# A fused attention and ReGLU block on one Trainium2 core: one load of activations cut into four pieces on two DMA queues

## The chip, the cores and the metric

The kernel runs on one core of one Trainium2 chip. A core has a matrix engine (TensorE, PE in the profile), a vector engine (VectorE, DVE), an engine for activations (ScalarE, ACT), GpSimd (POOL) and an engine that mainly issues DMAs (SyncE, SP). PEld is TensorE's weight load. Each engine works through its own list of instructions in order. The metric is the device time of one execution in microseconds (us), lower being better. The time before is 204.27 us, the median of 4 runs (202.77 to 205.07).

## The reference: what is computed

For 2048 rows x of 512 bf16 numbers, a layer norm, an attention with 32 heads of 16 numbers over 8 keys at distances 0, 2, ..., 14, a residual, a second layer norm and a gated feed-forward block with 1376 inner columns:

```
h  = x + A(layernorm(x), wqkv, wo)       # A: qkv = x @ wqkv; softmax over 8 dilated keys; @ wo
g  = layernorm(h) @ W_gate;  u = layernorm(h) @ W_up
h2 = h + (relu(g) * u) @ W_down
```

## The kernel before: stages, queues and order

The 2048 rows are four chunks of 512 rows (tk 0 to 3), and each chunk is four blocks of 128 rows (j 0 to 3). All of x lives in one tile `x_sm` with 16 blocks; chunk 1 is blocks 4 to 7. For each chunk the kernel takes the layer norm (statistics on VectorE at L419 and L422, the reciprocal root on ScalarE at L432 and L436, the normalised rows on VectorE at L454), transposes the rows (TensorE at L483 with evictions at L497 on VectorE and L499 on ScalarE, or by DMA at L472), multiplies with `wqk_sb` and `wv_sb` (L524, evicted by ScalarE at L532), does the attention (products on VectorE at L571 and L659 with additions by DMA at L691, sums and spreads on TensorE at L577 and L638), multiplies with `wo_sb` (L711), and does the feed-forward block (L749, L753, L756, L769, L786, L797).

The order of all this work on each engine is fixed: `Plan.order` sorts the steps by a list of ranks written out by hand (`RANK`), and nothing of it depends on when a load lands. Loads enter that plan only as assumed landing times. The loads themselves, and some constants, are emitted by `setup()`, ahead of every step of the plan. For the steps of this case, `setup()` puts out, in order of the program:

- four loads of 128 rows each for chunk 0, even blocks on SP's queue and odd blocks on ACT's (L282);
- the four 128-row slabs dt 0 to 3 of the query and key weights `wqk_sb`, even slabs on SP's queue and odd slabs on ACT's (L284);
- one load of 512 rows for chunk 1 on SP's queue (L285);
- the load of ScalarE's function table (L286), which stands on ScalarE's list after its four DMA issues;
- constants on GpSimd, then two copies of one number that act as gates: the copy at L299 reads the first block of chunk 0, and the load of `wv_sb` (L300) follows it; the copy at L301 reads the first block of chunk 1, block 4, and the load of chunk 2 (L303) follows it;
- on SP's queue then chunk 3 (L303), `wo_sb` (L305), `wu_sb` (L306), `wg_sb` (L307), `wd_sb` (L308, L311).

The tool that builds the program signals the landings of DMAs of both hardware queues (SP's and ACT's) on eight semaphores, taken in rotation in the order in which the DMAs stand in the program. A DMA therefore waits, on the engine that issues it, until the DMA eight places before it in that order has landed. In the program of before, places 1 to 8 are the four loads of chunk 0 (ACT's block 1, SP's block 0, ACT's block 3, SP's block 2) and the four slabs (dt 1, dt 0, dt 3, dt 2). The load of chunk 1 is place 9 and waits for block 1; `wv_sb` is place 10 and waits for block 0; chunk 2 and chunk 3 wait for blocks 3 and 2; `wo_sb` waits for dt 1, and so on.

On TensorE the list begins with 44 warm-up products (L373), the transposes of blocks 0 and 1, 16 filler products (L381), the first four products of L524 (one for each slab dt 0 to 3, on 256 columns), and the transposes of blocks 3 and 2 between further products. On VectorE the statistics of chunk 1 (L419) come after the eviction L497 of block 3; block 7 is the first of them, then blocks 6, 5 and 4.

Of the kernel before, what the change touches and what calls it, by code (L numbers as in the profile page):

```python
# [187 lines left out]
def kernel(  # L188
# [11 lines left out]
    nc = tc.nc  # L200
# [16 lines left out]
    BPC = CS // P  # L217
# [4 lines left out]
    x_rows = A_x.rearrange("b (tb p) d -> p (b tb) d", p=P)  # L222
# [20 lines left out]
    x_sm = sb.tile([P, NTB, D], BF16, name="x_sm")  # L243
# [34 lines left out]
    def setup():  # L278

        w3_r = A_wqkv.rearrange("(dt p) f -> p dt f", p=P)  # L280
        for j in range(BPC):
            (nc.scalar if j % 2 else nc.sync).dma_start(x_sm[:, j:j + 1, :], x_rows[:, j:j + 1, :])  # L282
        for dt in range(NT):
            (nc.scalar if dt % 2 else nc.sync).dma_start(wqk_sb[:, dt:dt + 1, :], w3_r[:, dt:dt + 1, 0:2 * D])  # L284
        nc.sync.dma_start(x_sm[:, BPC:2 * BPC, :], x_rows[:, BPC:2 * BPC, :])  # L285
        nc.scalar.preload_act_table_set("natural_log_exp_and_others")  # L286
        V.memset(warm[:], 0.0)
        make_identity(nc, identity[:])
        nc.gpsimd.memset(eps_t[:], EPS)
        nc.gpsimd.iota(ci[:], pattern=[[0, 1]], base=0, channel_multiplier=1)  # L290
        nc.gpsimd.iota(sel_i[:], pattern=[[1, H]], base=0, channel_multiplier=0)
        nc.gpsimd.iota(sp_i[:], pattern=[[1, H], [0, DQ]], base=0, channel_multiplier=0)
        nc.gpsimd.iota(sm_i, pattern=[[0, 4], [1, H]], base=0, channel_multiplier=0)
        nc.gpsimd.iota(mk_i[:], pattern=[[1, PADL]], base=0, channel_multiplier=0)
        nc.gpsimd.memset(kT[:, :, 0:PADL], 0.0)
        nc.gpsimd.memset(vT[:, :, 0:PADL], 0.0)


        nc.gpsimd.tensor_copy(out=wv_sb[0:1, 0, 0:1], in_=x_sm[0:1, 0, 0:1])  # L299
        nc.sync.dma_start(wv_sb[:], w3_r[:, :, 2 * D:3 * D])  # L300
        nc.gpsimd.tensor_copy(out=x_sm[0:1, 2 * BPC, 0:1], in_=x_sm[0:1, BPC, 0:1])  # L301
        for tk in range(2, NCK):
            nc.sync.dma_start(x_sm[:, tk * BPC:(tk + 1) * BPC, :], x_rows[:, tk * BPC:(tk + 1) * BPC, :])  # L303

        nc.sync.dma_start(wo_sb[:], A_wo.rearrange("(p t) f -> p t f", t=NT))  # L305
        nc.sync.dma_start(wu_sb[:], B_W_up.rearrange("(dt p) f -> p dt f", p=P))  # L306
        nc.sync.dma_start(wg_sb[:], B_W_gate.rearrange("(dt p) f -> p dt f", p=P))  # L307
        nc.sync.dma_start(  # L308
            wd_sb[:, 0:NFF, :], B_W_down[0:NFF * P, :].rearrange("(ft p) n -> p ft n", p=P))
        if FTAIL:  # L310
            nc.sync.dma_start(wd_sb[:FTAIL, NFF, :], B_W_down[NFF * P:F, :])  # L311


        for n, (op, by) in enumerate(((ALU.arith_shift_right, 2), (ALU.bitwise_and, H - 1),
                                      (ALU.arith_shift_right, 5))):
            V.tensor_scalar(out=tmp[:, n:n + 1], in0=ci[:], scalar1=by, scalar2=None, op0=op)
        V.tensor_copy(out=cf[:, 0:3], in_=tmp[:])
        V.tensor_scalar(out=cf[:, 2:3], in0=cf[:, 2:3], scalar1=1.0 * DIL, scalar2=None, op0=ALU.mult)
        V.tensor_scalar(out=cf[:, 3:4], in0=cf[:, 2:3], scalar1=4.0 * DIL, scalar2=None, op0=ALU.add)
        V.tensor_scalar(out=sel[:], in0=sel_i[:], scalar1=cf[:, 0:1], scalar2=None, op0=ALU.is_equal)  # L320
        V.tensor_scalar(out=spread[:], in0=sp_i[:], scalar1=cf[:, 1:2], scalar2=None, op0=ALU.is_equal)
        V.tensor_scalar(out=same[:], in0=sm_i, scalar1=cf[:, 1:2], scalar2=None, op0=ALU.is_equal)
        for hf in range(2):
            V.tensor_scalar(out=mask[:, hf, :], in0=mk_i[:], scalar1=cf[:, 2 + hf:3 + hf],
                            scalar2=None, op0=ALU.is_ge)
# [488 lines left out]
    with tc.manual_schedule():  # L814
        setup()
        for op in todo:
            if op.fn is not None:
                op.fn()
# [35 lines left out]
```

## Time and profile before

| what | value |
|---|---|
| median of 4 runs | 204.27 us (202.77 to 205.07) |
| the profiled execution's own time | 205.07 us |
| its span, first to last instruction | 203.3 us |
| mean granted TensorE clock | 0.994 |
| TensorE busy | 193.6 us, 95% of the span |
| VectorE busy | 153.3 us, 75% |
| ScalarE busy | 121.8 us, 60% |
| GpSimd busy | 12.7 us, 6% |
| load of chunk 1, issue to landing | 7.0 us |
| load of `wv_sb`, issue to landing | 7.9 us |

Lines such as L285 are line numbers of the kernel. In a timeline a row has the start, the busy time, the engine, the line, the operation, what it writes and reads, how many instructions were merged into the row, and in brackets how long the engine sat idle before it and what ended that. An engine name with a q (SPq, ACTq) is the engine's sequencer: it issues a DMA, and the time is that of the issue and not of the transfer. In the chain of work that ended last, each row has a start, a duration and what carried the chain then. A row of waits has the waiting instruction, what it waited for, the total in us, how many times, and the longest.

### The profile page before, as it was taken

The numbers are of one execution on the slowest core, as the hardware profiler recorded it, in microseconds if no ns is written. First come the engines' busy times: TensorE is split into PE (matmuls) and PEld (weight loads), VectorE is DVE, ScalarE is ACT, GpSimd is POOL, SyncE is SP. The second block draws the span as 40 slices with busy tenths as digits, with TensorE's granted clock in tenths as the row PEclk, the third lists the DMA queues.
The fourth block names the chain that finished last, engine by engine and source line by source line (L and its number), as shares of the span: only waits on it lengthen the run. The fifth ranks groups of instructions, "written<-read, shape, count | busy, mean of one in ns | idle before, by whom it ended". The sixth has DMA issues, their size and how long they took to land.

```text
span 203.3 us, 2938 instructions
## 1 busy us (share of the span) xinstructions
PE 193.6 (95%) x1095; PEld 96.1 (47%) x1115; DVE 153.3 (75%) x239; ACT 121.8 (60%) x256; POOL 12.7 (6%) x28
## 2 busy tenths in 40 slices
PE   8799999989999999999999999999999999999990
PEld 8576446545445434444444444444444444444460
DVE  6689998989999999999996768799958313023240
ACT  3367698746899966787436779601568511477300
POOL 3000000420000013100131000000000000000000
PEclk9999999999999999999999999999999999999997
DMA  5969962895000009920399400221010130200103
GB/s 150 351 193 380 401 191 53 150 206 108 3 0 0 0 3 175 194 44 3 63 177 191 118 0 0 50 53 55 0 52 0 26 77 3 77 0 0 52 6 100
DMA packets 17677, 18.83 MB, mean 93 GB/s; under 512 B 8352, under 2 KB 14464, under 8 KB 17664
## 3 DMA queue, kind: packets, MB, share of 16 engines
q1 hardware_dynamic: 15360, 11.57, 18.4%
q0 software_dynamic: 1728, 6.29, 16.4%
q10 hardware_dynamic: 576, 0.79, 1.4%
q8 instruction: 9, 0.15, 0.3%
q14 instruction: 4, 0.03, 0.0%
HBM read 8.42 MB, written 2.10 MB: 52 GB/s over the span
## 4 chain that ended last, share of the span: by engine, by line
PE 65%; DVE 15%; DMA 8%; ACT 5%; SPq 2%; issue 2%; ACTq 0%
PE bank L749 28%; PE bank L524 15%; PE bank L786 14%; DVE big L659 6%; PE bank L711 5%; DMA quad<-row 4%; DMA wqk_sb<-in_A_wqkv_dram 4%; DVE big L571 3%; DVE gT L769 2%; SPq L472 1%; DVE x_sm L722 1%; DVE big L662 1%; PE bank L577 1%; PE bank L483 1%; ACT big L644 1%
## 5 line engine op out<-in xcount | busy, mean ns | idle before, releaser
L749 PE MATMUL bank<-quad,wu_sb 128*128 128x512 bf16 (+1 forms) x172 | 42.4, 379 | 0.4
L749 PE MATMUL bank<-quad,wg_sb 128*128 128x512 bf16 (+1 forms) x173 | 42.0, 379 | 0.3 <-DMA quad<-row 0.3
L756 ACT ACTIVATE gr<-bank 128x512 bf16<-128x512 f32 (+1 forms) x44 | 25.4, 618 | 24.7 <-PE bank L749 22.9
L786 PE MATMUL bank<-wd_sb,gT 128*128 128x512 bf16 (+2 forms) x183 | 39.8, 366 | 0.2
L753 ACT CAST up_sb<-bank 128x512 bf16<-128x512 f32 (+1 forms) x44 | 25.1, 602 | 21.0 <-PE bank L749 17.3
L571 DVE TENSOR_TENSOR big<-quad,kT 128x4096 bf16<-128x4096 bf16 x16 | 36.2, 2285 | 0.2
L659 DVE TENSOR_TENSOR big<-big,vT 128x4096 bf16<-128x4096 bf16 x16 | 35.9, 2282 | 0.0
L769 DVE TENSOR_TENSOR gT<-gr,up_sb 128x1024 bf16<-128x1024 bf16 (+1 forms) x24 | 15.3, 642 | 24.0 <-ACT up_sb L753 14.4
L524 PE MATMUL bank<-quad,wqk_sb 128*128 128x512 bf16 (+1 forms) x139 | 30.2, 355 | 2.1 <-DMA wqk_sb<-in_A_wqkv_dram 1.0
L786 PEld LDWEIGHTS <-gT 128*128 128x128 bf16 (+1 forms) x187 | 18.1, 98 | 19.7 <-issue 0.4
L749 PEld LDWEIGHTS <-wg_sb 128*128 128x128 bf16 (+1 forms) x176 | 17.3, 100 | 21.1 <-issue 0.9
L749 PEld LDWEIGHTS <-wu_sb 128*128 128x128 bf16 (+1 forms) x176 | 17.5, 100 | 20.6 <-issue 0.7
L524 PEld LDWEIGHTS <-wqk_sb 128*128 128x128 bf16 x144 | 15.6, 114 | 14.1 <-issue 2.4
L797 DVE TENSOR_TENSOR row<-x_sm,bank 128x512 bf16<-128x512 bf16 (+1 forms) x17 | 10.6, 649 | 10.4 <-PE bank L786 10.4
L644 ACT CAST big<-bank 128x512 bf16<-128x512 f32 x32 | 17.8, 641 | 0.4 <-PE bank L638 0.2
L662 DVE TENSOR_TENSOR big<-big 128x1024 bf16<-128x1024 bf16 (+2 forms) x24 | 16.8, 728 | 0.1
L691 POOL DMA_DIRECT2D big<-big x12 | 10.5, 872 | 87.9 <-DVE big L659 59.9
L524 PE MATMUL bank<-quad,wv_sb 128*128 128x512 bf16 x62 | 15.6, 380 | 0.2
L711 PE MATMUL bank<-wo_sb,quad 128*128 128x512 bf16 x62 | 15.2, 379 | 0.2
L454 DVE TENSOR_SCALAR row<-x_sm,mv,rs 128x512 bf16<-128x512 bf16 x32 | 11.4, 407 | 3.7 <-ACT rs L436 3.1
L499 ACT COPY quad<-bank 128x1024 bf16<-128x1024 bf16 (+1 forms) x9 | 8.0, 931 | 7.2 <-PE bank L483 7.2
L532 ACT CAST quad<-bank 128x512 bf16<-128x512 f32 x16 | 9.5, 614 | 4.6 <-PE bank L524 4.6
(68 smaller groups left out, 147.2 us busy)
## 6 DMA issues: line engine op xcount, KB each, us to landing
big<-big POOLq DMA_DIRECT2D x12, 512.0 KB, 5.5
out_dram<-row SPq DMA_DIRECT2D x15, 128.0 KB, 1.8
x_sm<-in_A_x_dram SPq DMA_DIRECT2D x3, 512.0 KB, 5.8
wu_sb<-in_B_W_up_dram SPq DMA_DIRECT2D x1, 1376.0 KB, 9.7
wg_sb<-in_B_W_gate_dram SPq DMA_DIRECT2D x1, 1376.0 KB, 12.8
wd_sb<-in_B_W_down_dram SPq DMA_DIRECT2D x1, 1280.0 KB, 16.0
wqk_sb<-in_A_wqkv_dram ACTq DMA_DIRECT2D x2, 256.0 KB, 6.5
wqk_sb<-in_A_wqkv_dram SPq DMA_DIRECT2D x2, 256.0 KB, 6.7
```

The lines of the kernel that those rows point to most:

```text
L454: V.tensor_scalar(out=xn.t[:], in0=x, scalar1=mv.t[:, j, 0:1], scalar2=rs.t[:, j:j + 1], op0=ALU.add if residual else ALU.subtract, op1=AL ...
L524: nc.tensor.matmul(mm.t[:, lo:hi], lhsT=wv_sb[:, dt, t:D:NT] if c == 2 else wqk_sb[:, dt, c * D + t:(c + 1) * D:NT], rhs=xnT.t[:, dt, lo:h ...
L571: V.tensor_tensor(out=pb.t[:].rearrange("p (t w) s -> p t w s", t=2), in0=q4, in1=k4, op=ALU.mult)
L644: nc.scalar.copy(out=ab.t[:, w, :], in_=bc.t[:])
L659: V.tensor_tensor(out=mt.t[:], in0=ab.t[:], in1=v8, op=ALU.mult)
L662: V.tensor_tensor(out=mt.t[:, 0:n, :], in0=mt.t[:, 0:n, :], in1=mt.t[:, n:2 * n, :], op=ALU.add)
L711: nc.tensor.matmul(od.t[:], lhsT=OT.t[:, t, j * P:(j + 1) * P], rhs=wo_sb[:, t, :], start=(t == 0), stop=(t == NT - 1 and tk not in RPE))
L749: nc.tensor.matmul(mm.t[:fs, :], lhsT=w_sb[:, dt, ft * P: ft * P + fs], rhs=hnT.t[:, dt, :], start=(dt == 0), stop=(dt == NT - 1))
L753: nc.scalar.copy(out=ub.t[:fs, i, :], in_=um.t[:fs, :])
L756: nc.scalar.activation(out=gr.t[:fs, i, :], in_=gm.t[:fs, :], func=ACT.Relu)
L769: V.tensor_tensor(out=gt.t[:fs, 0:n, :], in0=gr.t[:fs, 0:n, :], in1=ub.t[:fs, 0:n, :], op=ALU.mult)
L786: nc.tensor.matmul(od.t[:, c0:c1], lhsT=gts[ft].t[:fs, ft % 2, j * P:(j + 1) * P], rhs=wd_sb[:fs, ft, c0:c1], start=(ft == 0), stop=(ft == ...
```

## The change

The single load of chunk 1 is replaced by four loads of one block (128 rows, 128 KB) each. Blocks 4 and 6 go to SP's queue and blocks 5 and 7 to ACT's. The place in `setup()` is the same: after the slabs of `wqk_sb` and before the table load. The bytes are the same, and nothing else of the kernel is edited.

```
@@ -282,7 +282,8 @@
             (nc.scalar if j % 2 else nc.sync).dma_start(x_sm[:, j:j + 1, :], x_rows[:, j:j + 1, :])
         for dt in range(NT):
             (nc.scalar if dt % 2 else nc.sync).dma_start(wqk_sb[:, dt:dt + 1, :], w3_r[:, dt:dt + 1, 0:2 * D])
-        nc.sync.dma_start(x_sm[:, BPC:2 * BPC, :], x_rows[:, BPC:2 * BPC, :])
+        for j in range(BPC, 2 * BPC):
+            (nc.scalar if j % 2 else nc.sync).dma_start(x_sm[:, j:j + 1, :], x_rows[:, j:j + 1, :])
         nc.scalar.preload_act_table_set("natural_log_exp_and_others")
         V.memset(warm[:], 0.0)
         make_identity(nc, identity[:])
```

More of the change, by code (lines that the diff above doesn't have):

```diff
@@ L284, in setup @@
             (nc.scalar if dt % 2 else nc.sync).dma_start(wqk_sb[:, dt:dt + 1, :], w3_r[:, dt:dt + 1, 0:2 * D])
-        nc.sync.dma_start(x_sm[:, BPC:2 * BPC, :], x_rows[:, BPC:2 * BPC, :])
+        for j in range(BPC, 2 * BPC):
+            (nc.scalar if j % 2 else nc.sync).dma_start(x_sm[:, j:j + 1, :], x_rows[:, j:j + 1, :])
         nc.scalar.preload_act_table_set("natural_log_exp_and_others")
```

## The prediction, made before the change was run

> **What bounds the kernel now.** I read the chain of work that ended last first, since the change touches only the first 20 us and the question is what carries the end there.
>
> ```profile
> 2.16 7.12 DMA wqk_sb<-in_A_wqkv_dram
> 9.28 0.05 issue
> 9.32 0.41 PE bank L524 x2
> 9.73 0.22 PE bank L483 x4
> ...
> 31.49 0.86 PE bank L524 x4
> 32.35 0.24 PE bank L483 x4
> 32.59 0.03 issue
> 32.62 0.42 DVE row L454
> ```
>
> The load of slab dt 2, issued by SP at 2.16, lands at 9.28 and starts TensorE's third product of L524. From there to 32.6 every row is TensorE's but for hops of 0.05, so whatever moves that product moves everything up to there; the chain then goes on through work in a fixed order to the end. No row names the load of chunk 1.
>
> Next the timeline from 0 to 20 us, for what stands around that load:
>
> ```profile
> 2.61 1.28 ACT L286 ACT_TABLE_LOAD   x1 [2.61 <-issue]
> ...
> 3.45 0.39 SPq L285 DMA_DIRECT2D x_sm<-in_A_x_dram  x1
> ...
> 3.95 0.46 SPq L300 DMA_DIRECT2D wv_sb<-in_A_wqkv_dram  x1
> ...
> 4.63 0.29 ACT L432 ACTIVATE rs<-mv,eps_t 128x1 f32<-128x1 f32 x1 [0.73 <-DVE mv L422]
> ...
> 6.83 1.06 PE L381 MATMUL bank<-warm 128*128 128x128 bf16 x16
> ...
> 7.92 0.41 PE L524 MATMUL bank<-quad,wqk_sb 128*128 128x256 bf16 x2
> ...
> 9.32 0.41 PE L524 MATMUL bank<-quad,wqk_sb 128*128 128x256 bf16 x2 [0.99 <-DMA wqk_sb<-in_A_wqkv_dram]
> ...
> 9.99 0.42 DVE L497 COPY quad<-bank 128x512 bf16<-128x512 bf16 x1 [1.56 <-PE bank L483]
> ...
> 10.51 2.47 DVE L419 BATCH_NORM_STATS2 st<-x_sm 128x6 f32<-128x512 bf16 x4
> 10.54 0.18 POOL L301 COPY x_sm<-x_sm 1x1 bf16<-1x1 bf16 x1 [6.71 <-DMA x_sm<-in_A_x_dram]
> ...
> 10.74 1.41 SPq L303 DMA_DIRECT2D x_sm<-in_A_x_dram  x2
> ```
>
> Three things are in it. The load of chunk 1 lands at 3.45 + 7.0 = 10.45; its reader, L419, starts at 10.51, directly behind L497 (9.99 + 0.42 = 10.41), with no idle time noted. So the landing and VectorE's arrival coincide, and VectorE's arrival was set by TensorE, which was set by dt 2. TensorE has a hole of 0.99 us before 9.32, and VectorE one of 1.56 before 9.99: chunk 0's layer norm is early by about 1 us. And ScalarE's table load starts at 2.61, as its fourth DMA issue ends; the first layer norm step of chunk 0 on ScalarE follows at 4.63, 0.73 after the table load.
>
> Last the waits of SP's queue:
>
> ```profile
> SPq L285 <- DMA x_sm<-in_A_x_dram: 0.8, 1, 0.8
> ```
>
> L285 reads nothing that an earlier load writes, yet SP stood 0.8 us, until block 1 (issued 0.73, 2.7 to landing: 3.43) was there. That is the wait for the DMA eight places earlier, at work.
>
> [...] slabs of both queues land together (dt 1 at 1.64 + 6.0 = 7.64, dt 0 at 1.69 + 6.2 = 7.89, dt 3 at 2.13 + 6.9 = 9.03, dt 2 at 9.28). [...]
>
> **The change part by part.**
>
> Removed: one issue on SP (0.39). Added: two issues on SP and two on ACT, at 0.40 to 0.46 each by the like-sized loads of chunk 0. Three DMAs more in the rotation.
>
> *ACT.* Blocks 5 and 7 are among places 9 to 12 and wait for chunk 0's blocks, on ScalarE's list ahead of the table load. Block 5 waits for block 1 or 0 (3.43 or 0.74 + 2.9 = 3.60), block 7 for block 3 or 2 (1.16 + 2.9 = 4.04, or 1.20 + 3.1 = 4.26). I take ACT first in each pair, as in the first eight places: block 7 issues at 4.06 + 0.45 = 4.51, the table load runs 4.54 to 5.82, L432 starts at 5.85 instead of 4.63: 1.22 late. With the other order it is 6.07, 1.44 late. Everything of chunk 0's layer norm queues behind it. From 5.85: L432 and L436 of block 0 take 0.53 (4.63 to 4.96 plus 0.20), so L454 of block 0 at 6.43; block 1's pair ends 0.45 later, L454 of block 1 from 6.88 to 7.28 (0.40). TensorE's transposes of block 1 take 0.36 and a hop of 0.06, to 7.70; the fillers 0.94, to 8.64. VectorE meanwhile does L422 (block 3), L419 (0.66), L422 (block 2), then L497 of block 1 from 8.09 to 8.48. ScalarE's L499 of block 0 ends by about 8.2. So L524 starts at 8.68 instead of 7.92, its first two products end at 9.09, and the third waits for dt 2 as before, to 9.32. The hole of 0.99 covers it with 0.23 left; in the late case the start is 8.90, the end 9.31, and nothing is left. L454 of blocks 3 and 2 end at about 8.9 and 9.3; their transposes stand at 9.57 and 10.23. Cost: 0. Without that cover it would be 0.76 us.
>
> *SP.* Block 4 issues at 3.45 to 3.62, block 6 at about 4.06 to 4.28. `wv_sb` moves from place 10 to 13 and waits for place 5, dt 1: issue at 7.7 instead of 3.95. [...] I put its landing at 12 to 12.5 instead of 11.8 (the worst bound is 7.7 + 7.9 = 15.6). Its first product is at 17.42, so the cost is 0. Chunk 2, 3 and `wo_sb` wait for dt 0, dt 3 and dt 2, all landed by 9.28; the later weights wait for the pieces themselves. From place 21 on, each DMA has the same partner as before.
>
> *Landing.* The same bytes lie behind the same slabs: block 7, the first that L419 reads, should land at 10.2 to 10.5 and block 4 near 9.7. L419 stays at about 10.51, since L497 holds VectorE until 10.41. If block 7 is late by d, VectorE is late by d; it has 0.57 of idle time, waiting for TensorE, at 32.62, and TensorE's transposes of chunk 1 at 16.31 come 2 us after the first L454 row, so up to about 0.5 us is hidden.
>
> *Gate L301.* It needs block 4 alone: 9.8 instead of 10.54, so chunk 2 issues at 10.0 instead of 10.74, and all later loads about 0.75 earlier. Chunk 2 now lands at 10.74 + 3.4 = 14.1 and is first read at 15.16 (L419): early already. Gain 0.
>
> Sum: the profiled span stays 203.3. That execution took 205.07, or 1.77 more than its span, and lies 0.80 above the median of the runs. I put the same zero on the median: 204.27, say 204.3.
>
> **Rivals.**
>
> *ScalarE's delay is longer than the hole (slower).* The place is L432. The hole covers 1.44 us of delay; past that the end moves one for one. For it: two more issues, two waits and a table load now stand in series ahead of the only engine that can start chunk 0. Against it: landings of chunk 0 are 2.7 to 3.1 us after issue and hardly move, as all lie before anything the change touches. [...] To cost 1% it would have to be 2.3 us later than I put it.
>
> *dt 2 lands earlier (faster).* `wv_sb`'s 512 KB are no longer in flight before 7.7, and the DMA engines are busy without a hole then. But TensorE is ready for the third product only at 9.09, so the gain is capped at 0.23: 204.0. [...]
>
> *Block 7 lands 1.5 us late (slower),* [...] the 0.5 that is hidden leaves 1.0: 205.3. [...]
>
> *The pieces start chunk 1 earlier (faster).* Excluded by L497 at 9.99: VectorE is not free before 10.41, and TensorE not before its own list allows.
>
> **How the numbers follow.** Hidden altogether, within 0.15 us: 0.72, at 204.3. Late ScalarE, +0.2 to +1.4: 0.13. Late block 7: 0.05. Early dt 2: 0.10. A measurement of this kernel tells about 1%, 2.0 us, from no change, and every case lies within that; what is left is the scatter of runs, 202.8 to 205.1 before, and something unseen. Faster by over 1%: 0.04, within 1%: 0.88, slower by over 1%: 0.08. The range takes in early dt 2 and the late cases (205.4) with 1.1 and 0.4 us of scatter: 202.9 to 205.8.
>
> **What would show it.** Right: the table load at about 4.5 and L432 at 5.8 to 6.1; L300 issued near 7.7, and L303 near 10.0; TensorE's hole before the third product down from 0.99 to 0.0 to 0.25, and that product still at 9.3, the chain still entering through the slab. Wrong: a chain that enters through L432 or L454 on its way to TensorE before 10 us, an idle wait of VectorE before L419 at 10.5, or a wait of L524 for `wv_sb`.

## The result and the profile after

The changed kernel takes 204.80 us (median of 35 runs, 203.39 to 206.41), the kernel before 203.92 us (56 runs, 202.63 to 205.96). The ratio is 1.0034, with a 95% interval of 1.0017 to 1.0051: slower by about 0.7 us (the two medians lie 0.88 us apart), well inside the 1% that was called no change, but not nothing. Ratios here and below leave out the executions that lie over 1.5% above the fastest of the same kernel, while the counts of executions below take in all of them.

The profiled executions say the opposite at first sight: a span of 201.7 us after, against 203.3 before. Most of that is the end. TensorE's last product ends at 197.97 after and at 198.35 before; the other 1.2 us lie in the landing of the last two stores (see the last section). One execution is not the median, so the 0.7 us has to be sought in many.

The chain after still enters through slab dt 2, 0.12 us earlier than before. Line numbers from L286 on are higher by one.

```profile
2.16 6.99 DMA wqk_sb<-in_A_wqkv_dram
9.15 0.05 issue
9.20 0.41 PE bank L525 x2
```

Three rows of the timeline before that the prediction does not show, needed for what follows:

```profile
0.99 4.87 PE L373 MATMUL bank<-warm 128*128 128x128 bf16 x44 [0.99 <-DVE warm L287]
...
6.27 0.72 PE L483 MATMUL bank<-identity,row 128*128 128x128 bf16 x8 [0.41 <-DVE row L454]
...
15.16 0.69 DVE L419 BATCH_NORM_STATS2 st<-x_sm 128x6 f32<-128x512 bf16 x1
```

The timeline after:

```profile
0.99 4.67 PE L374 MATMUL bank<-warm 128*128 128x128 bf16 x44 [0.99 <-DVE warm L288]
...
4.19 1.28 ACT L287 ACT_TABLE_LOAD   x1 [4.19 <-DMA x_sm<-in_A_x_dram]
...
5.48 0.29 ACT L433 ACTIVATE rs<-mv,eps_t 128x1 f32<-128x1 f32 x1
...
6.51 0.82 PE L484 MATMUL bank<-identity,row 128*128 128x128 bf16 x8 [0.85 <-DVE row L455]
...
9.20 0.41 PE L525 MATMUL bank<-quad,wqk_sb 128*128 128x256 bf16 x2 [0.60 <-DMA wqk_sb<-in_A_wqkv_dram]
...
15.63 0.69 DVE L420 BATCH_NORM_STATS2 st<-x_sm 128x6 f32<-128x512 bf16 x1 [0.69 <-DMA x_sm<-in_A_x_dram]
```

The table load stands at 4.19 instead of 2.61 and waits for a block of chunk 0, as forecast; L433 is 0.85 us late. TensorE's hole before the third product has shrunk from 0.99 to 0.60. But its other hole, ahead of the first transposes, has grown from 0.41 to 0.85. VectorE now waits 0.69 us for chunk 2 at 15.63, which it did not before. SP's waits:

```profile
SPq L301 <- DMA wqk_sb<-in_A_wqkv_dram: 2.6, 1, 2.6
```

That is `wv_sb`, moved from place 10 to place 13 of the rotation and issued at 7.72, 0.09 us behind the landing of dt 1 (7.63), place 5. The two traces show the rotation itself: the landings of both queues' DMAs, 48 before and 51 after, are signalled on eight semaphores, six to each before, and seven on three of them after. And the pieces, places 9 to 12, were issued at 3.27, 3.44, 3.82 and 4.68, each 0.02 us behind the landing of the DMA eight places earlier (3.25, 3.42, 3.80 and 4.66).

### The profile page after: what moved, and what is told of

It reads as the page before. It is cut to its first block, busy times and chain, and to the rows that moved or that the text cites. A ratio compares the mean times of both kernels' runs of the same rounds, so it can differ in the third digit from the quotient of the medians.

```text
span 201.7 us, 2941 instructions
## 1 busy us (share of the span) xinstructions
PE 193.5 (96%) x1095; PEld 96.1 (48%) x1115; DVE 153.2 (76%) x239; ACT 121.8 (60%) x256; POOL 12.7 (6%) x28
## 4 chain that ended last, share of the span: by engine, by line
PE 66%; DVE 15%; DMA 8%; ACT 5%; SPq 2%; issue 2%; ACTq 0%
PE bank L750 29%; PE bank L525 15%; PE bank L787 14%; DVE big L660 6%; PE bank L712 5%; DMA quad<-row 4%; DMA wqk_sb<-in_A_wqkv_dram 3%; DVE big L572 3%; DVE gT L770 2%; SPq L473 2%; DVE x_sm L723 1%; DVE big L663 1%; PE bank L578 1%; PE bank L484 1%; ACT big L645 1%
## 5 line engine op out<-in xcount | busy, mean ns | idle before, releaser
L692 POOL DMA_DIRECT2D big<-big x12 | 10.5, 872 | 88.2 <-DVE big L660 59.7
```

## The experiments

Each kernel was timed against the kernel before on the same chip. For each execution the list of runs has the span and the mean granted TensorE clock, the share of the full clock that the trace's clock record grants over the span. Half clock for 3.4 us, as a trace below has it, takes 0.008 off this mean, as an estimate (1.7 of about 203 us). Half clock after TensorE's last product counts too (in the profile of before it stands from 200.77 to the end at 203.3 and makes the 0.994), while the slow start, ahead of the first full clock, does not (in the changed kernel's own profile the full clock came at 5.31, and the mean is 1.000). In this list the changed kernel falls into two groups: 17 of its 36 executions have a mean clock of 0.985 to 0.990 and a mean span of 203.3 us, the others 0.994 to 1.000 and 202.2 us. A mean clock of 0.990 or less is called a low clock below. Three sources of the loss were open: ScalarE's delay by itself, VectorE's wait for chunk 2, and the landing of the last stores.

**The changed kernel again.**

> The changed kernel once more, to have its ratio on the same chip as the three beside it and a second trace. Every theory: about 1.003 (0.7 us slower). Theory ScalarE (chunk 0's layer norm is 0.8 to 1.2 us late, and in some executions the hole before TensorE's third product does not cover it): the third product at 9.2 to 9.8 in the trace. Theory chunk 2 (its load lands 1.4 us later, VectorE waits for it at 15.6, and its idle time at 32.5 is used up): VectorE waits 0.5 to 0.9 us for x_sm at 15.6. Theory tail (the last stores land 1.2 us or 2.0 to 3.4 us after issue, by whether a 16 KB packet of the instruction queue falls on them): TensorE ends within 0.3 us of 198.0, and the span is about 201.7 or about 203.2, by the landing of the last two stores.

Measured: 1.0036 (1.0015 to 1.0056). 8 of 22 executions had a mean clock of 0.990 or less, and none of the 75 of before beside them. The trace shows a hole of 1.16 us ahead of the transposes, no wait before the third product (8.67), TensorE's end at 197.44 and a span of 201.2. The loss is there again, and this single execution does not show it either. Theory tail misses: TensorE's end lies 0.56 us ahead of its 198.0, and the last two stores took 1.6 us, as in every profile but that of before.

**Table load ahead of the pieces.**

```
         for dt in range(NT):
             ...
+        nc.scalar.preload_act_table_set("natural_log_exp_and_others")
         for j in range(BPC, 2 * BPC):
             (nc.scalar if j % 2 else nc.sync).dma_start(x_sm[:, j:j + 1, :], x_rows[:, j:j + 1, :])
-        nc.scalar.preload_act_table_set("natural_log_exp_and_others")
```

> The changed kernel with ScalarE's table load ahead of the two pieces on ScalarE's queue. All is as in the changed kernel, but the table load starts at 2.6 again and L432 at about 4.7. Theory ScalarE: ratio 1.000, the loss of 0.7 us is gone. Theory chunk 2: 1.003, with VectorE's wait for x_sm near 15.6. Theory tail: TensorE's end within 0.3 us of 198.0 and the ratio by the tail alone, 1.000 to 1.005.

Measured: 0.9996 (0.9973 to 1.002), 2 low clocks of 22. The table load is back at 2.61; L433, at 5.04, still waits for the issue of block 7. No loss shows although all four pieces remain (the interval still allows 0.4 us), so the way to it seems to lead through ScalarE. Why two low clocks are left is not known.

**Pieces on SP's queue alone.**

```
         for j in range(BPC, 2 * BPC):
-            (nc.scalar if j % 2 else nc.sync).dma_start(x_sm[:, j:j + 1, :], x_rows[:, j:j + 1, :])
+            nc.sync.dma_start(x_sm[:, j:j + 1, :], x_rows[:, j:j + 1, :])
```

> The four pieces all on SP's queue, so that ScalarE issues none of them: table load at 2.6, L432 at 4.6, while the later loads stand in the rotation as in the changed kernel (wv_sb issued near 7.7). Theory ScalarE: ratio 1.000. Theory chunk 2: 1.003. Theory tail: TensorE's end within 0.3 us of 198.0 and the ratio by the tail, 1.000 to 1.005.

Measured: 1.0032 (1.0014 to 1.005), and no low clock in 22 executions. A miss for theory ScalarE, which wanted 1.000: this kernel has a loss of its own without the low clocks. By the ratio it is 0.65 us, as large as that of the changed kernel; the medians, 204.13 against 203.84 us, lie only 0.3 us apart (0.88 and 0.85 for the changed kernel).

**wv_sb issued behind chunk 2.**

```
-        nc.sync.dma_start(wv_sb[:], w3_r[:, :, 2 * D:3 * D])
         nc.gpsimd.tensor_copy(out=x_sm[0:1, 2 * BPC, 0:1], in_=x_sm[0:1, BPC, 0:1])
         for tk in range(2, NCK):
             nc.sync.dma_start(x_sm[:, tk * BPC:(tk + 1) * BPC, :], x_rows[:, tk * BPC:(tk + 1) * BPC, :])
+            if tk == 2:
+                nc.sync.dma_start(wv_sb[:], w3_r[:, :, 2 * D:3 * D])
```

> The changed kernel with the load of wv_sb issued behind that of chunk 2 instead of ahead of it. Chunk 2 should land near 14, ahead of its first reader, and VectorE's wait of 0.69 us before 15.63 goes; wv_sb lands near 15.5, ahead of 17.4. Theory chunk 2: ratio 1.000. Theory ScalarE: 1.003. Theory tail: TensorE's end within 0.3 us of 198.0 and the ratio by the tail, 1.000 to 1.005.

Measured: 1.005 (1.0024 to 1.0075), 9 low clocks of 22. VectorE's wait for chunk 2 is gone (chunk 2 landed at 14.68, L421 for it at 15.79 with no wait), and the loss is not: theory chunk 2 falls. By luck this profile caught a low clock. Its TensorE rows:

```profile
0.99 3.94 PE L375 MATMUL bank<-warm 128*128 128x128 bf16 x44 [0.99 <-DVE warm L288]
6.80 1.03 PE L485 MATMUL bank<-identity,row 128*128 128x128 bf16 x8 [1.88 <-DVE row L456]
```

The 44 warm-up products took 3.94 us here, 4.67 in the changed kernel's own profile and 4.87 before: the clock came up earlier in this execution, so the warm-up ended earlier, and with the rows late the hole is 1.88 us. In the profiles of before and after the warm-up products follow each other every 107 ns at first; after, the last of them, with the full clock granted, every 56 ns. In the traces' clock records the full clock is granted from 3.77 here and from 5.31 in the changed kernel's own profile; before it is from 6.21, behind the warm-up. Then, by the second, with TensorE's busy time, its granted clock, the DMA share and GB/s:

```profile
6.00:7.00 1.00, 0.20 (x4) 1.00 1.03 395
7.00:8.00 1.00, 0.98 (x12) 0.59 1.06 385
8.00:9.00 1.00, 1.00 (x12) 0.50 0.84 291
9.00:10.00 1.00, 1.00 (x10) 0.50 0.12 41
10.00:11.00 1.00, 1.00 (x10) 0.70 0.07 16
```

The clock is halved from 7.18 (a mean of 0.59 over 7 to 8) to 10.60 (0.70 over 10 to 11), for 3.4 us. The 16 fillers take 1.71 us in it (1.06 in the changed kernel's own profile), four products of L526 take 0.85 us (0.44 there), the third product starts at 9.76 instead of 9.20, and TensorE ends at 199.09 instead of 197.97. The chain of this execution no longer enters through a slab but through ScalarE and the rows, the sign of error that the prediction had named:

```profile
4.47 0.19 ACT L287
4.66 1.11 issue
5.77 0.30 ACT rs L434
...
6.33 0.42 DVE row L456
...
7.83 1.71 PE bank L383 x16
```

From the rise of the clock to its fall, 3.77 to 7.18, it is 3.4 us as well. TensorE was idle for 1.87 us of them, 55%, and the half clock followed. In the changed kernel's own profile the 3.4 us after the full clock came up, 5.31 to 8.72, were idle for 1.0 us, 29%, and the clock stayed full.

So a fourth theory, clock: ScalarE's delay widens the hole between warm-up and transposes; in executions where the clock came up early, the hole is long enough to halve it. The next kernels test it.

**More warm-up in the changed kernel.**

```
-    NWARM, NFILL = 44, 8
+    NWARM, NFILL = 56, 8
```

> The changed kernel with 56 warm-up products ahead of the first transposes instead of 44; ScalarE stays as late as in the changed kernel. Theory clock (a late L432 lengthens TensorE's hole between the warm-up and the transposes of block 0; where TensorE's clock came up early, so that the warm-up ended early, the hole is 1.9 us, and the clock is then halved for 3.4 us, about 1.4 us lost): 12 more products take 0.7 us at full clock, the hole is 1.2 us at most, the share of executions with a mean clock of 0.990 or less falls from 8 of 22 to 0 to 2, and the ratio to 1.000 to 1.002. Theory ScalarE (the late rows cost time by themselves): the share of low clocks tells nothing, the ratio stays 1.003 to 1.004.

Measured: 0.9992 (0.998 to 1.0004), no low clock in 22. ScalarE is as late as ever (table load at 4.32, block 0's transposes at 6.64), but in this trace the hole is closed; the transposes follow with no idle time noted on TensorE:

```profile
6.64 0.82 PE L484 MATMUL bank<-identity,row 128*128 128x128 bf16 x8
```

VectorE waits 1.04 us for chunk 2 in this trace, longer than in the changed kernel, and nothing is lost by it.

**ScalarE late in the kernel before.**

```
+    junk = sb.tile([P, 3, 2], BF16, name="junk")
         ...
         nc.sync.dma_start(x_sm[:, BPC:2 * BPC, :], x_rows[:, BPC:2 * BPC, :])
+        for n in range(3):
+            nc.scalar.dma_start(junk[:, n, :], x_rows[:, n, 0:2])
         nc.scalar.preload_act_table_set("natural_log_exp_and_others")
```

> The kernel before, its load of chunk 1 whole, with three loads of 4 bytes in each of 128 rows, into a tile that nobody reads, on ScalarE's queue ahead of the table load. They wait for blocks of chunk 0, so the table load starts near 4.6 and L432 near 5.9; the later loads stand three places on, as in the changed kernel. Theory clock and theory ScalarE: the loss is that of the changed kernel, ratio 1.003 to 1.006, with 6 to 10 of 22 executions at a mean clock of 0.990 or less by theory clock. Theory pieces (the four loads themselves cost it): 1.000.

Measured: 1.007 (1.0045 to 1.0095), 6 low clocks in 7 executions. The table load came at 5.38, later than I had put it, and the loss is larger than the changed kernel's. The profile has the hole and, from 8.54 to 11.95, the half clock:

```profile
7.70 0.82 PE L486 MATMUL bank<-identity,row 128*128 128x128 bf16 x8 [2.13 <-DVE row L457]
```

The pieces are not needed for a loss. How much of this one the clock makes is not told apart: ScalarE's first step (L435) stands at 6.67, 2.04 us late, beyond the 1.44 us that the prediction's hole covers, so late rows can cost here by themselves as well.

**Less warm-up in the kernel before, 36 and 28.**

```
-    NWARM, NFILL = 44, 8
+    NWARM, NFILL = 36, 8
```

The second kernel has 28 in the same place.

> The kernel before with 36 warm-up products instead of 44; no load and nothing on ScalarE is changed. Theory clock: 8 fewer products shorten the warm-up by 0.45 us at full clock and 0.85 at half, so the hole before the transposes is 0.9 to 1.8 us as in the changed kernel; low mean clocks (0.990 or less) in 3 to 10 of 22 executions, ratio 1.001 to 1.005, though the rows are as early as before. Theory ScalarE: the rows come when they came, ratio 1.000, with no low clocks beyond the 0 of 75 of before.

Measured with 36: 0.9982 (0.9968 to 0.9996), no low clock in 22; a miss. The hole in the trace is 1.02 us. I then measured 36 again and 28 beside it.

> The kernel before with 36 warm-up products a second time, for whether its 0.9982 of the first time holds: if a shorter warm-up helps, 0.996 to 0.9995 again; if that was scatter, 0.999 to 1.002. By theory clock, with holes up to about 1.7 us, 0 to 3 low clocks of 22.

Measured: 0.9987 (0.997 to 1.0003), none in 22, a hole of 1.14. So 0.9982 did not clearly hold, and the holes of about 1.1 us in these two traces did no harm.

> The kernel before with 28 warm-up products instead of 44, loads and ScalarE as before. With 36 no low clock came, so the hole there (about 1.0 us in the trace, up to 1.7 by the earliest rise of the clock) was still too short; with 28 it is 1.4 to 2.4 us. Theory clock: holes of 1.9 and 2.1 us were followed by the half clock, 1.0 and 1.2 were not, so low mean clocks (0.990 or less) return in 5 to 20 of 22, ratio 1.002 to 1.007. Without it: rows as early as before, 0.998 to 1.000.

Measured: 1.0011 (0.9989 to 1.0032), 4 of 22 at 0.990 or less and a fifth at 0.991, where the 51 executions of before had none. Low clocks do return with nothing on ScalarE touched, but fewer than I expected, and the time is not clearly longer. In the trace the hole is 1.96 us, but the full clock came only at 9.35, behind it, so there was nothing yet to halve. Such a late rise is not what the list counts as a low clock: this execution's mean is 0.996.

**Late rows and less warm-up together:** the changed kernel with this edit.

```
-    NWARM, NFILL = 44, 8
+    NWARM, NFILL = 36, 8
```

> The changed kernel with 36 warm-up products instead of 44: late rows and a short warm-up together. Theory clock: the hole is 0.45 to 0.85 us longer than in the changed kernel, so the share of low clocks rises from 8 of 22 to 11 to 20 of 22, ratio 1.004 to 1.008. Theory ScalarE (late rows alone): 1.003 to 1.004 as with 44.

Measured: 1.0032 (1.0006 to 1.0059), 4 of 14 at 0.990 or less, 6 at 0.991 or less; the profile has a hole of 2.33 us, and the half clock from 7.08 to 10.5. A miss in size: the share of low clocks did not rise clearly over the changed kernel's 25 of 58. With 14 executions it is known only roughly, and how the share follows from the hole stays open.

**Pieces on SP's queue and wv_sb behind chunk 2.** Both edits above in one kernel, to find the 0.3 us of the pieces on SP's queue.

> Pieces all on SP's queue, and wv_sb issued behind chunk 2: neither ScalarE's delay nor VectorE's wait for chunk 2 at 15.5. No low clocks are expected by any theory. Theory chunk 2 (the 0.3 us that the kernel with all pieces on SP's queue lost without one low clock is VectorE's wait for chunk 2): ratio 1.000. Without it: 1.001 to 1.003 as there.

Measured: 1.0012 (0.9992 to 1.0032), medians of 204.31 against 203.90 us; nobody waits for chunk 2 (L420 for it at 15.26). The ratio doesn't tell the two apart. Where the loss of the pieces on SP's queue goes is not settled; the changed kernel with the table load ahead or with 56 warm-up products shows none.

## Why the prediction was right, and where it was not

The forecast of no change within 1% held, and so did the range. The time, 204.3 with no loss, missed a loss of 0.7 us.

*What bounds the kernel* held. TensorE's third product waits for dt 2 in the profile after as in that of before (9.20 and 9.32). The other traces say it more strongly: slab dt 2 landed anywhere from 8.00 (table load ahead) to 9.72 (56 warm-up products), and TensorE's last product ended 188.8 to 189.2 us after that landing in all ten traces without a half clock inside the work. In the three with one it ended 189.75 to 190.5 us after. So much of the scatter between single traces is that landing, and the half clock, late rows included, cost about 0.7 to 1.5 us.

*ACT, cost 0* is the step that failed. The delay itself was right in kind and a little too large in size (table load 4.54 forecast, 4.19 and 4.42 measured; L432 5.85 forecast, 5.48 and 5.72 measured). Its cover was right in kind too: in the profiled execution TensorE's hole before the third product took it, with 0.60 left where 0.23 was forecast. What I left out is that TensorE has two holes there. I followed the rows through the transposes and asked only when the next product is late; I did not ask what the idle time ahead of the transposes does, which the same timeline showed as 0.41 us before, and which the same sum puts at 1.0 after (from 5.86 to 6.43 + 0.40 + 0.06 = 6.89). A hole hides work, but it is also idle time, and in three traces TensorE's clock fell behind holes of 1.88, 2.13 and 2.33 us. The sum of it, as an estimate: 25 of 58 executions of the changed kernel (17 of 36 and 8 of 22) had the low clock, with a mean span of 203.35 us, 1.5 above the 201.83 of the 75 executions of before beside its second measurement. 1.5 us in 43% of executions is 0.65 us, against 0.7 measured. That close a fit is partly chance. In the second measurement, over the executions that count in its ratio, 5 low clocks of 18 make 0.4 us; the other 13 were 0.45 us longer than before in the mean, though not in the median, and make the other 0.3. Whether those 0.3 are more than scatter, the interval of 0.3 to 1.1 us does not say. A direct part, rows that set the third product where dt 2 lands early (as in the second trace of the changed kernel, 8.67 with no wait), can be little: with 56 warm-up products the rows are as late, and the upper end of the interval is 1.0004, or 0.1 us.

Shown: filling the hole takes the loss and the low clocks away with ScalarE as late as ever (0.9992, none of 22), and having the table load ahead takes away all or most of both (0.9996, 2 of 22). The kernel before loses time once ScalarE is late (1.007), and gets low clocks with its hole lengthened alone (28 products). Not explained: the loss without low clocks when all pieces are on SP's queue, where ScalarE is early. Only argued: that it is the early rise of the clock that picks the executions. The traces agree as far as they go: three caught the drop, and in them 55, 63 and 68% of the 3.4 us after the full clock came up was idle. In the ten without the drop it was 38% at most, the one with 28 products among them, whose hole of 1.96 us came before the full clock did.

*The rival of a late ScalarE* (0.13, 204.5 to 205.4) named the right engine and nearly the right time with the wrong mechanism. It had the end move once L432 passes 1.44 us of delay; the loss comes with delays of 0.85 to 1.1 us, as in the traces of the changed kernel, and the half clock in some executions only. The 205.4 allowed for more delay behind the table load; none shows, as L433 at 5.48 stands 0.01 us behind the end of that load (4.19 + 1.28 = 5.47).

*SP* held: `wv_sb` issued at 7.72 (7.7 forecast) and landed at 12.16 (12 to 12.5, an estimate), and cost nothing.

*Landing* held in part. The loads of both queues landed in the order of their issue in both profiles: blocks of chunk 0 from 3.43 to 4.26, slabs from 7.65 to 9.28, chunk 1 at 10.49, `wv_sb` at 11.81 and chunk 2 at 14.19 before, and with the pieces as with the one load chunk 1 came behind the slabs, the last of them at 9.15. Blocks 5, 4, 7 and 6 landed at 9.37, 9.88, 10.06 and 10.32, and L420 started at 10.21, 0.34 us behind the start of L498, where it had been 0.52 (9.99 to 10.51). So before, it had waited about 0.2 us for the landing, with no idle time noted, and the pieces do bring the statistics of chunk 1 forward by that. I see no gain from it: the transposes of chunk 1, at 16.40 after and 16.53 before, stand where TensorE's list puts them, and moved by about as much as the third product did.

*Gate L301* was wrong in its second half. Chunk 2 was issued at 10.14 (10.0 forecast), but landed at 15.60 rather than before 14.1: 5.5 us after its issue, where it had taken 3.4. `wv_sb`, issued late, was ahead of it, and that is a part of it: with `wv_sb` behind it took 4.7 us (10.00 to 14.68). I had carried the old latency over to a queue that was no longer empty. VectorE's wait of 0.69 us came out of its idle time before 32.5 (0.3 left of 0.57), and the kernel with 56 warm-up products shows 1.04 us of it at no cost.

*dt 2 earlier, block 7 late:* the first is within 0.1 us in the profile after (9.15 against 9.28), but the landing was 8.52 in the changed kernel's second trace and 8.00 with the table load ahead, against 9.08 to 9.50 in the five traces with chunk 1 in one load. That is suggestive and no more, as with 56 warm-up products it was 9.72. The cap of 0.23 us on such a gain was wrong: the third product started at 8.67 in the second trace, 0.65 us ahead of the 9.32 of before, so TensorE was ready earlier than the 9.09 of the sum. Block 7 was not late (10.06, with 10.2 to 10.5 forecast); the 1.5 us of that rival was an estimate.

No version clearly beats the kernel before; the pieces with the table load ahead of them are as fast as the one load, within 0.4 us.

## What to carry to other kernels

A wait that is put in front of an engine's first work is not free just because the next consumer waits for something else: look at every hole of TensorE that the delay widens (from 0.41 to 0.85 us in the profile after), since idle time can also cost the clock behind it. Here the clock was halved for 3.4 us where 55% or more of the 3.4 us after its rise was idle, and not where 38% or less was; what lies between was not seen. Where a loss of a few tenths of a per cent shows in the median and not in a profile, list the executions by span and granted clock before looking for it in one trace. When a DMA is added, count what it does to every later DMA in the rotation and to the queue of the engine that issues it (three more moved `wv_sb` from 3.95 to 7.72 here, and the table load from 2.61 to 4.19), and don't carry an old latency over to a queue that has been reordered (chunk 2 took 5.5 us instead of 3.4).

## What was not expected of the hardware

Besides the half clock of 3.4 us behind 3.4 us that were 55 to 68% idle: the last two stores, 64 KB each, took 3.2 us to land in the profile of before and 1.6 in that of after. In the former a packet of 16 KB on the instruction queue lies in the same stretch, 198.5 to 202.5:

```profile
q8 instruction: 1, 0.02, 2.1%
...
out_dram<-row SPq DMA_DIRECT2D x2, 64.0 KB, 3.2
```

In the profiles of all the other kernels the two stores take 1.6 us. That the packet delays them is an inference from this one coincidence; no run tried it. It is the reason why the span of before (203.3 us) is no measure for the change.
